# Input transposes of a and b side by side on two 64-row tiles of TensorE, 4 KB rows, and a part of the gate products on GpSimd: one change to a tuned scan and mixture-of-adapters kernel

## The chip, the cores and the metric

The kernel runs on one core of one Trainium2 chip. The metric is the device time of one execution in microseconds (us). One execution of each kernel was also taken with a profile; its "span" is the time from the first to the last instruction of the core, about 2 us less than the device time. In its lines PE is TensorE and PEld its weight load, DVE is VectorE, ACT ScalarE, POOL GpSimd and SP the engine that issues the transfers; a q marks the sequencer of an engine, which waits and issues. SBUF is the on-chip memory, whose tensors have up to 128 partitions in these kernels, and PSUM is the memory into which their matmuls write. The "granted clock" is the share of its full clock that the profile records for TensorE. Executions have a faster and a slower state, and only fast runs are compared here. A kernel that was run only once has the state "unknown"; it is used where the effect is many times the scatter of the runs, and marked where it is not.

## The reference

Two inputs `a` and `b` of 8 x 6400 x 128 float32 are scanned along the 6400 positions. The 51200 resulting rows `x` of 128 values then go through a mixture of eight rank-16 adapters, of which each row uses its two best.

```python
h = np.zeros((B, D))
for t in range(S):                 # scan: h = a*h + b, for 8 sequences
    h = a[:, t] * h + b[:, t]
    out[:, t] = h
x = out.reshape(B * S, D)          # 51200 x 128
logits = x @ w_gate                # 8 experts
topk = np.argpartition(-logits, 2, axis=1)[:, :2]
w = softmax of the two selected logits
delta[rows of e] += w * ((x @ A[e]) @ B[e])      # rank 16
return x + delta
```

## The kernel before

The rows are worked on in 100 units of 512 tokens. The scan is written with time along the free dimension and the 128 channels on the partitions, but the inputs lie in memory with a token's 128 channels together. So each unit goes through these steps; the letters are used throughout:

- A and B: TensorE transposes the unit's `a` and `b` (4 + 4 float32 matmuls against an identity, 128 x 128 each). ScalarE copies `a` from PSUM to SBUF.
- scan: VectorE runs the scan, which writes `xT` in float16.
- L: TensorE computes the logits (4 matmuls with 8 columns). GpSimd and VectorE compute the gates for a group of units.
- Z: TensorE computes x·A for all eight experts at once (4 matmuls). The product of Z with the gates runs on VectorE.
- T: TensorE transposes the product; R adds x into the output's PSUM tile and D adds the product times B. ScalarE copies the result, and a DMA stores it.

In L, Z and R the *stationary* operand, which TensorE loads as weights, is a block of `xT`. Partition p of a load holds four consecutive tokens, so a block consists of every fourth token, and its weight load reads `xT` with a step of 4 elements, which is 8 bytes.

All operations are listed with their dependences, and a small list scheduler inside the kernel puts them in order on each engine. The numbers in `KEY` are sort keys that were tuned for the kernel before.

```python
Q = 4; UT = 128 * Q; RING = 16            # 4 tokens a row, 512 tokens a unit
...
# load: one transfer over 128 partitions, two units, runs of 2 KB
ring[:, s0 : s0 + n, :],
rows[u0 * UT : (u0 + n) * UT, :].rearrange("(n p i) d -> p n (i d)", p=128, i=Q),
...
# A, B: four full transposes each
view = dst[:, :].rearrange("d (p i) -> d i p", i=Q)
for i in range(Q):
    last = h.transpose(view[:, i, :], ring[:, w % RING, i * 128 : (i + 1) * 128], ident_f[:, :])
...
def x_block(w, i):                        # weights of L, Z and R
    x0 = (w % XR) * UT
    return xT[:, x0 : x0 + UT].rearrange("d (p i) -> d i p", i=Q)[:, i, :]
...
for i in range(Q):                        # L; Z and R look alike
    last = h.matmul(pL[:, c : c + E], x_block(w, i), wg_h)
```

## Time and profile before

| | before |
|---|---|
| time, median of 3 runs | 211.31 us (211.17 to 211.38) |
| span of the profiled run | 209.4 us |
| busy: TensorE / VectorE / ScalarE / GpSimd | 97% / 92% / 81% / 42% |
| DMA rate from 60 to 180 us | 398 GB/s |
| TensorE time for a unit, 60 to 180 us | 1.91 us |

The TensorE time for a unit is, here and below, TensorE's busy time in the stretch, divided by the number of its matmuls there and multiplied by the matmuls of a unit (28 before, 36 after).

From the page of the kernel before come these lines: the busy times (PEld overlaps PE: 202.2 and 194.9 us in a span of 209.4), the moved GB/s in 40 equal slices of the span, the DMA queue of loads and stores (packets, MB, share of the 16 engines' time), and the chain of waits by engine.

```profile
PE 202.2 (97%) x2842; PEld 194.9 (93%) x2842; DVE 193.6 (92%) x279; ACT 170.2 (81%) x356; POOL 87.1 (42%) x190
...
GB/s 172 388 387 385 389 383 386 385 391 392 398 391 394 399 396 398 401 396 403 391 403 397 399 403 397 398 404 391 398 405 397 405 395 397 402 400 344 237 269 269
...
q1 hardware_dynamic: 40848, 78.65, 99.8%
...
PE 87%; DVE 6%; ACT 2%; issue 2%; POOL 0%; DVEq 0%; POOLq 0%
```

TensorE, VectorE and the DMA queue are all nearly full. The chain that ended last is TensorE for 87%. The DMA reaches its rate in the second slice and keeps it until nearly 190 us.

The next lines are groups of instructions of the kernel before: line, engine, operation, output and inputs, count | busy us, mean ns of one | idle time ahead and what ended it. The first is the transposes of `a`. The others are weight loads: those of R (L598), Z (L521) and L (L406) read `xT`, and that of D (L610) reads `zwT`.

```profile
L350 PE MATMUL pA<-ident_f,a_in 128*128 128x128 f32 x400 | 62.2, 279 | 0.8 <-ACT a_st L364 0.6
...
L598 PEld LDWEIGHTS pO<-ident_h,xT 128*128 128x128 f16 x400 | 30.1, 114 | 0.6 <-ACT outt L626 0.3
L610 PEld LDWEIGHTS pO<-cst_h,zwT 128*128 128x128 f16 x400 | 27.3, 98 | 2.3 <-PE pO L598 0.9
L521 PEld LDWEIGHTS pZ<-cst_h,xT 128*128 128x128 f16 x400 | 28.7, 114 | 0.2
...
L406 PEld LDWEIGHTS pTL<-cst_h,xT 128*128 128x128 f16 x400 | 20.5, 117 | 0.8 <-DVE xT L381 0.8
```

The DMA issues of the kernel before (KB each, median us from issue to landing):

```profile
a_in<-in_a_dram SPq DMA_DIRECT2D x49, 512.0 KB, 11.4
b_in<-in_b_dram SPq DMA_DIRECT2D x49, 512.0 KB, 11.4
```

### The profile page before, as it was taken

To read this page: it belongs to the slowest core of one execution; us is meant where nothing else is said; L and a number is where in the kernel's file an instruction comes from. 1 tells how busy PE (TensorE), PEld (TensorE's weight loads), DVE (VectorE), ACT (ScalarE), POOL (GpSimd) and SP (SyncE) were. 2 spreads that over 40 slices of the span, in tenths; PEclk is the share of its full clock that TensorE was granted. 3 is DMA by queue.
4 is the path that set the end of the run, shared out by engine and by line. 5 is a ranking of instruction groups with operands and counts; after the bars stand their busy time and mean duration, and the time that the engine had idled before them with its cause. 6 is when DMAs were issued, how large, how long until landed. Compare 5 with 4: busy or idle time off the path is not lost.

```text
span 209.4 us, 7147 instructions
## 1 busy us (share of the span) xinstructions
PE 202.2 (97%) x2842; PEld 194.9 (93%) x2842; DVE 193.6 (92%) x279; ACT 170.2 (81%) x356; POOL 87.1 (42%) x190
## 2 busy tenths in 40 slices
PE   6989999999999999999999999999999999999992
PEld 4779899999999999999999999999999999999991
DVE  1599999999999999999999999999999999999980
ACT  2437587779888889978979789988998899899993
POOL 1032715063335443563362545435453654354310
PEclk9999999999999999999999999999999999999999
DMA  7999999999999999999999999999999999999677
GB/s 172 388 387 385 389 383 386 385 391 392 398 391 394 399 396 398 401 396 403 391 403 397 399 403 397 398 404 391 398 405 397 405 395 397 402 400 344 237 269 269
DMA packets 42208, 79.23 MB, mean 378 GB/s; under 512 B 3648, under 2 KB 3776, under 8 KB 42176
## 3 DMA queue, kind: packets, MB, share of 16 engines
q1 hardware_dynamic: 40848, 78.65, 99.8%
q8 instruction: 22, 0.36, 0.7%
q10 hardware_dynamic: 1328, 0.14, 0.5%
q14 instruction: 10, 0.08, 0.1%
HBM read 52.56 MB, written 26.21 MB: 376 GB/s over the span
## 4 chain that ended last, share of the span: by engine, by line
PE 87%; DVE 6%; ACT 2%; issue 2%; POOL 0%; DVEq 0%; POOLq 0%
PE pA L350 20%; PE pB L350 19%; PE pO L610 11%; PE pZ L521 10%; PE pO L598 10%; PE pTL L571 10%; DVE xT L381 6%; PE pTL L406 5%; ACT a_st L364 1%; ACT outt L626 1%; PE pB L300 0%; PE pB L303 0%; ACT zwT L590 0%; PE pA L571 0%; PE pB L312 0%
## 5 line engine op out<-in xcount | busy, mean ns | idle before, releaser
L381 DVE TENSOR_TENSOR_SCAN xT<-a_st,xT,pB 128x512 f16<-128x512 f32 x96 | 120.2, 1252 | 2.7 <-PE pB L350 1.1
L364 ACT COPY a_st<-pA 128x512 f32<-128x512 f32 x100 | 59.7, 597 | 18.0 <-PE pA L350 10.7
L555 DVE TENSOR_TENSOR zw<-pZ,g 128x512 f16<-128x512 f32 x100 | 66.9, 674 | 0.8 <-ACT a_st L364 0.2
L626 ACT COPY outt<-pO 128x512 f32<-128x512 f32 x98 | 57.8, 594 | 10.5 <-PE pO L610 9.1
L350 PE MATMUL pA<-ident_f,a_in 128*128 128x128 f32 x400 | 62.2, 279 | 0.8 <-ACT a_st L364 0.6
L350 PE MATMUL pB<-ident_f,b_in 128*128 128x128 f32 x400 | 61.7, 277 | 0.2
L590 ACT COPY zwT<-pTL 128x512 f16<-128x512 f16 x95 | 56.5, 595 | 3.5 <-PE pTL L571 1.9
L350 PEld LDWEIGHTS pB<-ident_f,b_in 128*128 128x128 f32 x400 | 44.1, 142 | 1.8 <-issue 1.1
L350 PEld LDWEIGHTS pA<-ident_f,a_in 128*128 128x128 f32 x400 | 43.3, 143 | 1.8 <-issue 1.3
L610 PE MATMUL pO<-cst_h,zwT 128*128 128x128 f16 x400 | 38.8, 219 | 0.4
L598 PE MATMUL pO<-ident_h,xT 128*128 128x128 f16 x400 | 38.7, 219 | 0.1
L521 PE MATMUL pZ<-cst_h,xT 128*128 128x128 f16 x400 | 38.6, 219 | 0.0
L571 PE MATMUL pTL<-ident_h,zw 128*128 128x128 f16 x380 | 36.7, 219 | 0.0
L598 PEld LDWEIGHTS pO<-ident_h,xT 128*128 128x128 f16 x400 | 30.1, 114 | 0.6 <-ACT outt L626 0.3
L610 PEld LDWEIGHTS pO<-cst_h,zwT 128*128 128x128 f16 x400 | 27.3, 98 | 2.3 <-PE pO L598 0.9
L521 PEld LDWEIGHTS pZ<-cst_h,xT 128*128 128x128 f16 x400 | 28.7, 114 | 0.2
L571 PEld LDWEIGHTS pTL<-ident_h,zw 128*128 128x128 f16 x380 | 25.7, 98 | 0.3
L406 PE MATMUL pTL<-cst_h,xT 128*128 128x8 f16 x400 | 22.0, 174 | 0.3 <-DVE xT L381 0.3
L406 PEld LDWEIGHTS pTL<-cst_h,xT 128*128 128x128 f16 x400 | 20.5, 117 | 0.8 <-DVE xT L381 0.8
L449 POOL TENSOR_TENSOR d_1<-Lg,m_1 128x128 f32<-128x128 f32 (+2 forms) x13 | 5.1, 390 | 32.6 <-DVE m_1 L441 32.6
L449 POOL TENSOR_TENSOR d_0<-Lg,m_0 128x128 f32<-128x128 f32 (+1 forms) x12 | 4.8, 398 | 29.4 <-DVE m_0 L441 29.4
L381 DVE TENSOR_TENSOR_SCAN xT<-a_st,pB 128x512 f16<-128x512 f32 (+1 forms) x8 | 7.5, 942 | 5.7 <-PE pB L350 5.4
(58 smaller groups left out, 129.9 us busy)
## 6 DMA issues: line engine op xcount, KB each, us to landing
a_in<-in_a_dram SPq DMA_DIRECT2D x49, 512.0 KB, 11.4
b_in<-in_b_dram SPq DMA_DIRECT2D x49, 512.0 KB, 11.4
out_dram<-outt SPq DMA_DIRECT2D x49, 512.0 KB, 11.4
a_in<-in_a_dram SPq DMA_DIRECT2D x2, 256.0 KB, 3.6
b_in<-in_b_dram SPq DMA_DIRECT2D x2, 256.0 KB, 4.0
out_dram<-outt SPq DMA_DIRECT2D x2, 256.0 KB, 2.6
cst_f<-in_moe_A_dram ACTq DMA_DIRECT2D x1, 64.0 KB, 3.9
cst_f<-in_moe_B_dram ACTq DMA_DIRECT2D x1, 64.0 KB, 4.5
```

Source lines behind the costliest of these rows:

```text
L350: last = h.transpose(view[:, i, :], ring[:, w % RING, i * 128 : (i + 1) * 128], ident_f[:, :])
L364: lambda h: h.copy(a_st[w % 2][:, :], pA[:, :]),
L381: last = h.tensor_tensor_scan(out=xT[:, x0 + lo : x0 + hi], data0=a_st[w % 2][:, lo:hi], data1=pB[w % 2][:, lo:hi], initial=init, op0=ALU. ...
L406: last = h.matmul(pL[:, c : c + E], x_block(w, i), wg_h)
L449: lambda h: h.tensor_tensor(out=v(d1[s]), in0=v(Lg[s]), in1=bc(m1[s]), op=ALU.subtract),
L521: last = h.matmul(pZ[w % NZ][:, i * 128 : (i + 1) * 128], x_block(w, i), Acat_h)
L555: lambda h: h.tensor_tensor(out=oview, in0=zview, in1=gview, op=ALU.mult),
L571: last = h.transpose(t_dst(w)[:, i * 128 : (i + 1) * 128], zw[w % 2][:, i, :], ident_h[:, :])
L590: lambda h: h.copy(zwT[w % 2][:, :], t_dst(w)),
L598: last = h.matmul(pO[w % NO][:, i * 128 : (i + 1) * 128], x_block(w, i), ident_h[:, :], start=i == 0, stop=False, skip_group_check=True,)
L610: last = h.matmul(pO[w % NO][:, i * 128 : (i + 1) * 128], zwT[w % 2][:, i * 128 : (i + 1) * 128], Bcat_h, start=False, stop=True, skip_gro ...
L626: return copy(outt[:, w % NOUT, :], pO[w % NO][:, :])
```

## The change

The intent: a float32 transpose of 64 x 64 on one half of TensorE's rows runs beside another one on the other half. The warm-up of the kernel before shows it: at 2.72 us and at 2.73 us two of them start on the two halves, and the next two at 2.83 us. If unit w's `a` lies on one half of the partitions and its `b` on the other, `a` and `b` are transposed at the same time, in about half the time. For that a row holds 8 tokens (4 KB) instead of 4, a pair of units fills the 128 partitions, and `b` is loaded into the half opposite to `a`. VectorE, the next fullest engine (92%), hands 26 of the 100 gate products to GpSimd; GpSimd's product is written to read Z from SBUF, so ScalarE copies it there first. The sort keys were tuned anew. This is the core of the diff, with cuts marked:

```diff
-    Q = 4
-    UT = 128 * Q
-    RING = 16
+    Q = 8
+    HQ = Q // 2
+    UT = 64 * Q
+    RING = 8
...
+    ON_POOL = lambda v: 8 < v < NU - 12 and v % 3 == 1
...
+        def load(n):
+            s0 = n % RING
+            la = [(a_in[64 * h : 64 * h + 64, s0, :], a_rows[n, h, :, :]) for h in range(2)]
+            lb = [(b_in[64 - 64 * h : 128 - 64 * h, s0, :], b_rows[n, h, :, :]) for h in range(2)]
...
+            if n < 2:
+                for h in range(2):
+                    add_dma(f"ld{2 * n + h}", "sp", unit + h, [la[h], lb[h]], ("i", n, h), size, old)
+            else:
+                whole = (a_in[:, s0, :], a_rows[n].rearrange("h p f -> (h p) f"))
+                add_dma(f"lda{n}", "sp", unit, [whole], ("a", s0), size, old)
+                add_dma(f"ldb{n}", "sp", unit, lb, ("b", s0), size, old)
...
-                for i in range(Q):
-                    last = h.transpose(
-                        view[:, i, :], ring[:, w % RING, i * 128 : (i + 1) * 128], ident_f[:, :]
-                    )
+                for i in range(Q):
+                    c = slice(i * D, (i + 1) * D)
+                    for half, dst, ring in ((ha, da, a_in), (hb, db, b_in)):
+                        rows = slice(half, half + 64)
+                        last = h.transpose(dst[:, i, :], ring[rows, n, c], ident_f[rows, rows])
...
+        def x_block(v, q):
+            i = (v % 2) * HQ + q
+            return x_cols(v // 2).rearrange("d (p i) -> d i p", i=Q)[:, i, :]
+
+        def scanned(v):
+            return f"scan{v // 2 * 2 + 1}"
```

`lb` has two entries, so each `b` load is two transfers of 64 partitions, while `a` is one transfer of 128 (except for the first two pairs, which load both by halves). And `scanned` makes the output side of a unit wait for the scans of both units of its pair.

## The prediction

The 410 GB/s for rows of 4 KB, from which the 192 us of DMA time and with them the span of about 201 us come, was the author's estimate, and the kernel before had moved 398 GB/s. The sum for the main risk came to about 250 us. The 0.053 us of a pair is the 0.105 us of the warm-up scaled by full transposes, which in the trace of before start every 213 ns in the first 7.6 us and every 109 ns from 9 us on. A "change" (of mode) is one between 64-row transposes and matmuls on the whole array; the estimate of 0.1 us for it was from the 0.13 us of the warm-up.

> **What bounds the kernel now.** Three resources run nearly level. (1) DMA: the page's queue part gives 78.65 MB, busy 99.8%; the slices show 385 to 405 GB/s until about 185 us. In SP's timeline issues take 0.4 us at the start, 1.2 us later, and a transfer lands 11.4 us after issue: the queue is full. At 398 GB/s (stretch 60 to 140 us) one 512-token unit (0.786 MB) costs 1.97 us. (2) TensorE: the chain of waits is 87% PE; a unit costs 0.44 (A) + 0.44 (B) + 4 x 0.22 + 0.125 = 1.89 us. (3) VectorE: scan 1.19, product 0.60, reduces 0.13 = 1.93 us. ScalarE: 1.6 us per unit. After the last load (185 us) some 22 us of drain follow.
>
> **What the change does.**
> - TensorE: 16 half-height transposes in pairs replace 8 full ones. In the warm-up of before, a 64-row pair starts every 0.105 us[...], so 0.053 us warm: 8 pairs = 0.43 us instead of 0.88. [...]the warm-up shows about 0.13 us extra per change[...]. The order of instructions has 94 transpose groups, so 188 changes; at an estimated 0.1 us, 19 us. TensorE falls to about 1.65 us per unit.
> - VectorE loses 26 of 100 products (16 us): 1.77 us per unit. GpSimd gains 26, about 1.15 us each (estimate: 0.46 us for a quarter of the elements now), off the path. ScalarE gains 26 copies: 1.72 us.
> - DMA: same bytes, rows of 4 KB instead of 2 KB. A 2 KB packet takes 84 ns (packet records).[...]
>
> **On the critical path.** All engines drop below the DMA, so TensorE's gain of some 25 us is mostly hidden; DMA decides: 78.65 MB at 410 GB/s = 192 us, 2.5 us of start, and a drain that leaves about 7 us of DMA time unused (before: 12 us of the span in all). Span about 201 us, time about 203 us: 4% faster.
>
> **Main risk.** Each b load is two transfers of 64 partitions.[...] If both halves run at half rate throughout, [...]the kernel takes about 250 us[...]. I give a visible loss one chance in five.
>
> **What would show each step.** Right: transpose groups of about 0.45 us; PE's share of the chain well under 87%, with DMA waits in it; VectorE busy about 177 us, ScalarE 186, GpSimd 117; slices at 405 to 415 GB/s. Wrong: GB/s under 390 in the middle, b loads landing much later than a loads[...]; gaps over 0.15 us at mode changes (TensorE stays the limit); VectorE idle on GpSimd products; slices near 398 (packet size did not matter: about 207 us).
>
> **What would make it wrong.** [...]dearer mode changes, ScalarE becoming the limit, or a better drain (196).
>
> Time 203 us, range 196 to 218; faster 0.66, same 0.15, slower 0.19.

## The result, and the profile after

| | before | after |
|---|---|---|
| time, median | 211.27 us (4 runs beside it: 211.17 to 211.38) | 270.11 us (4 runs: 267.06 to 273.11) |
| fast runs of the changed kernel | | 267.06 and 268.13 us |
| ratio of fast runs, 95% interval | | 1.267 (1.262 to 1.271): slower |
| span of the profiled run | 209.4 us | 265.3 us |
| DMA rate from 60 to 180 us | 398 GB/s | 316 GB/s |

A ratio in this document is the mean time of one kernel's fast runs over that of the other's in the same rounds, so it is not quite the ratio of the quoted medians. Two of the four runs (273.11 and 272.08) fell in the slow state and are left out of it. The profiled run is the fastest one.

The same lines of the page, of the kernel after:

```profile
PE 217.3 (82%) x3605; PEld 196.2 (74%) x3605; DVE 185.0 (70%) x252; ACT 185.6 (70%) x380; POOL 111.4 (42%) x207
...
GB/s 136 217 258 273 263 245 246 232 261 284 305 250 311 335 326 300 349 339 322 351 314 300 312 361 324 308 300 324 325 350 351 332 329 349 369 387 330 214 250 233
...
q1 hardware_dynamic: 22576, 78.66, 97.6%
...
DMA 49%; PE 38%; SPq 7%; issue 3%; ACT 2%
```

The DMA queue is busy for 97.6% of a span that is 56 us longer, with the same 78.66 MB. So its engines are occupied all the time and move less: about 250 GB/s in the early slices, and only slowly more. TensorE fell from 97% to 82% busy, and the chain of waits is now half DMA.

The groups of the kernel after that answer to those shown of before, with one of the transposes and the new GpSimd product:

```profile
L362 PE MATMUL pA<-ident_f,a_in 64*128 64x64 f32 x800 | 78.7, 245 | 37.8 <-DMA a_in<-in_a_dram 27.9
...
L595 POOL TENSOR_TENSOR zw<-z_sb,g 128x512 f16<-128x512 f32 x26 | 27.6, 1061 | 45.9 <-PE pTL L611 16.7
...
L641 PEld LDWEIGHTS pO<-ident_h,xT 128*128 128x128 f16 x400 | 34.6, 152 | 2.4 <-ACT outt L673 0.2
L557 PEld LDWEIGHTS pZ<-cst_h,xT 128*128 128x128 f16 x400 | 34.4, 151 | 1.8 <-POOL d_0 L533 0.7
...
L443 PEld LDWEIGHTS pTL<-cst_h,xT 128*128 128x128 f16 x400 | 29.3, 162 | 0.7 <-DVE xT L407 0.2
L653 PEld LDWEIGHTS pO<-cst_h,zwT 128*128 128x128 f16 x400 | 27.6, 102 | 1.9 <-PE pO L641 0.6
```

TensorE waits 27.9 us for input loads ahead of its transposes of `a`; before, all its idle time there came to 0.8 us, and the wait named is for ScalarE. The weight loads from `xT` went from 114 to 117 ns up to 151 to 162 ns, while the contiguous one stayed near 100.

The DMA issues of the kernel after:

```profile
b_in<-in_b_dram SPq DMA_DIRECT2D x100, 256.0 KB, 17.5
out_dram<-outt SPq DMA_DIRECT2D x49, 512.0 KB, 18.7
a_in<-in_a_dram SPq DMA_DIRECT2D x48, 512.0 KB, 19.6
```

Everything lands late, the `a` loads a little later than the `b` loads. So the name in a wait ("DMA a_in") does not tell which transfer was the slow one: all of them are in one queue, q1.

The packet records give it a size. In the kernel before, a 2 KB packet takes 84 ns in the median (81 at the least) and 86.5 ns on average. In the kernel after, 4 KB packets take 156 ns at the least, 159 ns where nothing disturbs them (e2_b_whole below), but 213.7 ns on average, and a quarter take over 264 ns. The mean follows if the third of the packets that belongs to `b` takes double and the rest 159 ns: (159 + 159 + 318) / 3 = 212 ns. That is arithmetic on the sum; single packets were not told apart by their transfer.

Where the 55.9 us of span came from, by the starts of the transposes of unit 10 and of unit 99 in the traces:

| span, us | before | after | difference |
|---|---|---|---|
| up to unit 10 | 21.3 | 32.8 | +11.5 |
| unit 10 to unit 99 | 171.8 | 211.3 | +39.5 |
| unit 99 to the end | 16.3 | 21.1 | +4.8 |

### The profile page after: what moved, and what is told of

The parts are those of the page before. It is cut to its first block, busy times and chain, and to the rows that moved or that the text cites. A ratio compares the mean times of both kernels' runs of the same rounds, so it can differ in the third digit from the quotient of the medians.

```text
span 265.3 us, 8714 instructions
## 1 busy us (share of the span) xinstructions
PE 217.3 (82%) x3605; PEld 196.2 (74%) x3605; DVE 185.0 (70%) x252; ACT 185.6 (70%) x380; POOL 111.4 (42%) x207
## 3 DMA queue, kind: packets, MB, share of 16 engines
q1 hardware_dynamic: 22576, 78.66, 97.6%
## 4 chain that ended last, share of the span: by engine, by line
DMA 49%; PE 38%; SPq 7%; issue 3%; ACT 2%
DMA a_in<-in_a_dram 49%; PE pA L362 11%; SPq L267 7%; PE pO L641 6%; PE pZ L557 6%; PE pTL L611 5%; PE pO L653 5%; PE pTL L443 4%; PE pB L362 1%; ACT outt L673 1%; ACT zwT L633 1%; PE pA L611 0%; ACT Lg L476 0%; ACT g L550 0%
## 5 line engine op out<-in xcount | busy, mean ns | idle before, releaser
L362 PE MATMUL pA<-ident_f,a_in 64*128 64x64 f32 x800 | 78.7, 245 | 37.8 <-DMA a_in<-in_a_dram 27.9
L362 PEld LDWEIGHTS pA<-ident_f,a_in 64*128 64x128 f32 x800 | 63.9, 153 | 47.3 <-DMA a_in<-in_a_dram 32.4
L362 PE MATMUL pB<-ident_f,b_in 64*128 64x64 f32 x800 | 78.6, 245 | 0.1
L595 DVE TENSOR_TENSOR zw<-pZ,g 128x512 f16<-128x512 f32 x74 | 50.4, 682 | 26.1 <-PE pTL L611 23.3
L362 PEld LDWEIGHTS pB<-ident_f,b_in 64*128 64x128 f32 x800 | 63.9, 153 | 1.9 <-issue 1.9
L595 POOL TENSOR_TENSOR zw<-z_sb,g 128x512 f16<-128x512 f32 x26 | 27.6, 1061 | 45.9 <-PE pTL L611 16.7
L641 PE MATMUL pO<-ident_h,xT 128*128 128x128 f16 x400 | 45.1, 239 | 0.0
L611 PE MATMUL pTL<-ident_h,zw 128*128 128x128 f16 x380 | 39.5, 229 | 2.8 <-issue 2.1
L443 PE MATMUL pTL<-cst_h,xT 128*128 128x8 f16 x400 | 31.4, 200 | 0.7 <-issue 0.7
L443 PEld LDWEIGHTS pTL<-cst_h,xT 128*128 128x128 f16 x400 | 29.3, 162 | 0.7 <-DVE xT L407 0.2
L581 ACT COPY z_sb<-pZ 128x512 f32<-128x512 f32 x26 | 15.5, 594 | 0.4 <-PE pZ L557 0.4
## 6 DMA issues: line engine op xcount, KB each, us to landing
b_in<-in_b_dram SPq DMA_DIRECT2D x100, 256.0 KB, 17.5
a_in<-in_a_dram SPq DMA_DIRECT2D x48, 512.0 KB, 19.6
```

The lines of the kernel that those rows point to most:

```text
L362: last = h.transpose(dst[:, i, :], ring[rows, n, c], ident_f[rows, rows])
L443: last = h.matmul(pL[:, c : c + E], x_block(v, q), wg_h)
L595: lambda h: h.tensor_tensor(out=oview, in0=zview, in1=gview, op=ALU.mult),
L611: last = h.transpose(t_dst(v)[:, q * 128 : (q + 1) * 128], zw[v % 2][:, q, :], ident_h[:, :])
L641: last = h.matmul(pO[v % NO][:, q * 128 : (q + 1) * 128], x_block(v, q), ident_h[:, :], start=q == 0, stop=False, skip_group_check=True,)
```

## The experiments

The theory to begin with (theory P in the expectations): two transfers to opposite halves of the partitions are slow because of the partitions that each of them covers. Why these partitions should matter was the author's assumption; no trace shows it. The range 32 to 95, as large as a half but across both, is there to test the partition numbers alone. The rivals: the 4 KB rows or the memory's order of access; the larger number of transfers; TensorE's mode changes; GpSimd. Twelve kernels were run. All ratios are against the kernel before on the same chip, which took 210.9 to 211.7 us in all but one of its runs (213.6). Differences between two changed kernels go across chips in places, e6_blocks and e7_unpaired against e3_b_shift above all; the kernel before took the same time on these chips to 0.3 us in the median. Several of the expectations missed: e2_b_whole and e4_b_mid lay between the two ranges given for them, e3_b_shift and e11_order_a above both; e1_before_b_halves and e14_two_switches came out 2 to 3 us over theirs, and e6_blocks 0.2 us under.

### e2_b_whole: b as one transfer over 128 partitions

This kernel is wrong on purpose: the halves of `b` arrive swapped. Its instructions on the compute engines have the same order as those of the kernel after.

```diff
-                add_dma(f"ldb{n}", "sp", unit, lb, ("b", s0), size, old)
+                whole_b = (b_in[:, s0, :], b_rows[n].rearrange("h p f -> (h p) f"))
+                add_dma(f"ldb{n}", "sp", unit, [whole_b], ("b", s0), size, old)
```

> The changed kernel with each b load of a pair of units as ONE transfer of 128 partitions instead of two of 64. The order of instructions on PE, DVE, ACT and POOL is the same; the halves of b land swapped, so the result is wrong on purpose. Theory P ([...]the 4 KB packets double from 159 ns towards 318 ns): about 200 to 208 us, mean 4 KB packet 159 to 165 ns, 405 to 415 GB/s in the middle. Rival H (rows of 4 KB, or the HBM addresses they touch, are slow): stays at 260 to 270 us. Rival E (mode changes of TensorE, the products on GpSimd, or the ring of 8 pairs hold the pipeline): stays at 260 to 270 us, for those are untouched.

Measured: 228.0 us, 39 us less than the fastest run of the kernel after. The slices of its page:

```profile
GB/s 123 221 325 405 414 403 411 409 398 409 415 411 412 413 414 413 414 411 412 413 412 416 411 411 416 412 399 382 408 414 412 411 256 169 66 175 126 221 281 188
```

The rate in the middle is 411 GB/s, above the 398 of before, and 4 KB packets take 166.9 ns on average. So 4 KB rows are not the cause; they are even a little better. But 228 us is still 17 us more than before: a second loss lies beneath the first.

### e4_b_mid and e5_b_apart: the same two transfers, on the middle partitions or on the two halves

Both are wrong on purpose: `b` is loaded into two buffers, and the transposes read `a` in place of `b`. They differ in two lines and have the same order of instructions on every engine, the same number of transfers and the same bytes. e5_b_apart is the control.

```diff
 # e4_b_mid                                  # e5_b_apart
-(b_in[32:96, s0, :], b_rows[n, 0, :, :]),
-(b_lo[32:96, s0, :], b_rows[n, 1, :, :]),
+(b_in[64:128, s0, :], b_rows[n, 0, :, :]),
+(b_lo[0:64, s0, :], b_rows[n, 1, :, :]),
```

> The changed kernel with the two 64-partition b loads of each pair kept in number, size and HBM rows, but both put on partitions 32 to 95 (in two buffers)[...]. The transposes read a's buffer in place of b's (wrong result on purpose; b is loaded and waited for, and not read). Theory P: about 200 to 210 us, packets near 159 ns. Rival N (a transfer of 64 partitions or 256 KB, or twice as many transfers, is slow[...]): 260 to 270 us.

> Control of the run on partitions 32 to 95: the same kernel, order and buffers, but the two b transfers on partitions 64 to 127 and 0 to 63 as in the changed kernel. Theory P: 260 to 275 us, mean 4 KB packet over 200 ns. If it is as fast as its sibling, the edit (reading a's buffer, the extra buffer) removed the loss[...].

Measured: 232.65 us on partitions 32 to 95, and 273.57 us on 64 to 127 and 0 to 63. The slices of e4_b_mid and then of e5_b_apart:

```profile
GB/s 119 221 325 409 410 406 410 410 410 407 413 413 413 403 414 397 398 373 392 412 408 419 397 408 409 408 390 380 378 412 383 415 209 168 91 183 119 163 273 186
```

```profile
GB/s 137 218 250 270 259 252 238 223 274 259 298 241 300 333 311 335 341 318 315 314 314 330 326 345 344 323 289 323 333 322 320 297 283 308 343 386 333 206 204 262
```

The number of transfers, the size of each, the rows and the work of all engines are the same; only the partition numbers differ, and 41 us go with them. The mean 4 KB packet is 168.6 against 219 ns. From 60 to 180 us e4_b_mid moved 401 GB/s, against 411 in e2_b_whole. This settles the main cause: it is the partitions that one transfer covers, not that there are two transfers. Why such a pair on the two halves is slow was not shown.

### e1_before_b_halves: the cause alone, in the kernel before

Only the `b` loads of the kernel before are cut into two transfers of 64 partitions. The result is correct.

```diff
+                for lo in ((0, 128),) if t == "a" else ((64, 128), (0, 64)):
+                    p = slice(*lo)
...
-                            rows[...].rearrange("(n p i) d -> p n (i d)", p=128, i=Q),
+                            rows[...].rearrange("(n p i) d -> p n (i d)", p=128, i=Q)[p],
```

> The kernel before, whole, except that each b load is cut into two transfers, partitions 64 to 127 and then 0 to 63 (2 KB rows, same bytes, right result). Nothing else of the change is in it. Theory P[...]: clearly slower, 240 to 275 us, many 2 KB packets near 168 ns instead of 84. If the loss needs the 4 KB rows or another part of the change: 211 to 216 us.

Measured: 277.18 us, 66 us more than before. Its slices and its chain of waits:

```profile
GB/s 182 264 269 237 251 246 225 225 279 212 254 252 250 276 293 282 335 355 322 311 303 299 305 303 308 324 302 288 298 289 338 331 301 345 299 363 391 318 260 233
...
DMA 67%; PE 23%; SPq 4%; issue 2%; ACT 2%; DVE 0%; ACTq 0%
```

The slices have the shape of those of the kernel after: near 250 GB/s at first, then slowly more. The mean 2 KB packet is 115.3 ns; with the third of the packets at double time it would be (84 + 84 + 168) / 3 = 112. One part of the change, alone, costs at least as much as the whole change did (this is a single run of unknown state, so the 10 us more are not read). No mode change outside the warm-up, no GpSimd product and no 4 KB row is in this kernel.

### e3_b_shift: a correct kernel with whole `b` loads

If `b` is shifted by one unit, its first half-tile holds unit 0 alone, and from then on units 2m-1 and 2m lie together, on the halves where they are wanted. One transfer over 128 partitions then loads both.

```diff
-                add_dma(f"ldb{n}", "sp", unit, lb, ("b", s0), size, old)
+                load_b(n)
+        def load_b(m):
...
+                rows = b_units[2 * m - 1 : 2 * m + 1].rearrange("u p f -> (u p) f")
+                src, size = (b_in[:, m % RING, :], rows), 2 * UT * D * 4
```

> A correct repair: b's tiles are shifted by half a tile (512 tokens), so that one transfer of 128 partitions brings unit 2m-1 to partitions 0 to 63 and unit 2m to 64 to 127; a and b of a unit still lie in opposite halves. All of the change's other parts stay. Theory P: 198 to 206 us, faster than before by 3 to 6%, DMA at 405 to 415 GB/s and still the limit. If TensorE's mode changes or ScalarE limit the rest: 207 to 215 us with DMA slices under 400 GB/s.

Measured: 224.39 us (222.85 to 225.28), ratio 1.061 (1.056 to 1.067), correct. The stretch from 60 to 180 us of the kernels before, after and e3_b_shift, in this order (busy us and number of instructions of PE, PEld, DVE, ACT, POOL, then granted clock, DMA share, GB/s):

```profile
60.00:180.00 120.00, 120.00 (x1760) 118.77 (x1758) 118.03 (x164) 105.62 (x223) 57.31 (x116) 1.00 1.05 398
```

```profile
60.00:180.00 120.00, 102.14 (x1794) 93.44 (x1793) 88.25 (x112) 93.47 (x192) 62.90 (x110) 0.97 1.04 316
```

```profile
60.00:180.00 120.00, 119.96 (x2207) 111.72 (x2206) 106.66 (x134) 113.02 (x236) 73.93 (x128) 1.00 1.03 413
```

With the half transfers gone from this stretch, TensorE is full again, for 120 of 120 us, and the DMA moves 413 GB/s. A unit costs TensorE 1.96 us, against 1.91 before. So the side-by-side transposes did not make TensorE faster over a whole unit, and the chain that ended last is TensorE again:

```profile
PE 84%; DVE 6%; DMA 4%; SPq 2%; ACT 2%; issue 1%; DVEq 0%
```

By the starts of its instructions in this stretch, a unit consists of 8 pairs at 62 ns (0.50), of which the second starts 50 ns later than that (0.05), the two gaps at mode changes (0.19), R and Z with 8 matmuls at 62 to 63 ns (0.50), T and D with 8 at 56 ns (0.45) and L with 4 at 60 ns (0.24): 1.93 us, and the rest is waits and R and Z steps above their median. Before, the sum was 8 transposes at 109 ns (0.87), 16 matmuls at 56 ns (0.90) and L with 4 at 33 ns (0.13): 1.90 us. A gain of 0.37 us on the transposes is used up by 0.24 us of mode changes (the 0.19 and the 0.05 us at the second pair), 0.05 us or more on R and Z, and 0.11 us on L.

The timeline of TensorE in one unit of before and of e3_b_shift (start us, us, engine, line and operation, count) shows the steps:

```profile
100.93 0.39 PE L598 MATMUL pO<-ident_h,xT 128*128 128x128 f16 x4
101.16 0.27 PE L406 MATMUL pTL<-cst_h,xT 128*128 128x8 f16 x4
101.29 0.39 PE L521 MATMUL pZ<-cst_h,xT 128*128 128x128 f16 x4
```

```profile
100.46 0.22 PE L378 MATMUL pA<-ident_f,a_in 64*128 64x64 f32 x1
100.52 0.22 PE L378 MATMUL pB<-ident_f,b_in 64*128 64x64 f32 x1
100.52 0.22 PE L378 MATMUL pA<-ident_f,a_in 64*128 64x64 f32 x1
100.68 0.40 PE L627 MATMUL pTL<-ident_h,zw 128*128 128x128 f16 x4
...
101.14 0.36 PE L459 MATMUL pTL<-cst_h,xT 128*128 128x8 f16 x4
101.36 0.43 PE L657 MATMUL pO<-ident_h,xT 128*128 128x128 f16 x4
...
101.85 0.43 PE L573 MATMUL pZ<-cst_h,xT 128*128 128x128 f16 x4
102.21 0.27 PE L378 MATMUL pA<-ident_f,a_in 64*128 64x64 f32 x1
...
102.32 0.22 PE L378 MATMUL pA<-ident_f,a_in 64*128 64x64 f32 x1
...
102.39 0.22 PE L378 MATMUL pA<-ident_f,a_in 64*128 64x64 f32 x1
```

From one start to the next: the four L matmuls take 0.13 us before and 0.22 in e3_b_shift. A pair follows the last one after 0.06 us, but the first full-array matmul follows the last transpose only after 0.16 us. In the stretch the medians are 155 ns from a transpose to a full matmul (59 inside the transposes) and 156 ns from Z to a transpose (62 inside Z): each mode change costs about 95 ns in its gap, which is what the prediction had taken. One step later stands another 50 ns: the second pair of a group starts 112 ns after the first, every later one 62 ns after the last (102.21, 102.32 and 102.39 us above). So a unit pays 0.24 us for its two changes, which makes some 23 us for 94 groups of transposes. The warm-up of the kernel before shows it too, with 0.16 us to the second pair and 0.105 us from then on. (The busy times of a matmul, 0.2 to 0.4 us here, overlap and are not its cost.)

### e6_blocks: weights without a step

This kernel is e3_b_shift with contiguous weight blocks in L, Z and R. It is wrong on purpose: the blocks hold the wrong tokens. The order of instructions is the same on every engine.

```diff
-            return x_cols(v // 2).rearrange("d (p i) -> d i p", i=Q)[:, i, :]
+            return x_cols(v // 2)[:, i * 128 : (i + 1) * 128]
```

> The shifted-b repair (224.4 us), but each 128-column block of xT that TensorE loads as weights is contiguous instead of taken every 8th element (16 bytes); wrong result on purpose (rows permuted), same order of instructions on every engine. Theory S (8 tokens per partition row made the weight loads of L, Z and R slower: a logits matmul starts every 60 ns instead of 33, R and Z every 63 to 71 instead of 56): L back to 33 to 40 ns, R and Z to 56, about 0.2 us less TensorE time per unit, then the DMA at 413 GB/s limits at 1.90 us per unit: 214 to 220 us. Rival (the slower L, Z, R are an effect of mode changes or waits nearby): cadences stay and so does the time, 222 to 226 us.

Measured: 213.84 us, 10.5 us less than e3_b_shift. The weight loads from `xT` in e3_b_shift, and then in e6_blocks:

```profile
L573 PEld LDWEIGHTS pZ<-cst_h,xT 128*128 128x128 f16 x400 | 33.9, 150 | 1.0 <-DVE zw L611 0.2
...
L459 PEld LDWEIGHTS pTL<-cst_h,xT 128*128 128x128 f16 x400 | 29.1, 163 | 0.7 <-DVE xT L423 0.2
```

```profile
L573 PEld LDWEIGHTS pZ<-cst_h,xT 128*128 128x128 f16 x400 | 25.8, 99 | 3.6 <-issue 1.5
...
L657 PEld LDWEIGHTS pO<-ident_h,xT 128*128 128x128 f16 x400 | 24.6, 98 | 4.3 <-issue 1.3
```

They take 97 to 99 ns now, as every contiguous one. L matmuls start every 25 ns, R and Z every 56, and a unit costs TensorE 1.78 us. So the step of the weights is the second loss. The three steps side by side: contiguous 97 to 99 ns (e6_blocks), 8 bytes 114 to 117 ns (before), 16 bytes 150 to 163 ns (e3_b_shift). The L matmuls, of only 8 columns, started every 25, 33 and 60 ns there.

### e7_unpaired: is the pairing worth anything?

This kernel is e3_b_shift with the eight transposes of `a` first and then the eight of `b`, so that neighbours use the same half.

```diff
-                for i in range(Q):
-                    c = slice(i * D, (i + 1) * D)
-                    for half, dst, ring, slot in ((ha, da, a_in, n), (hb, db, b_in, m)):
+                for half, dst, ring, slot in ((ha, da, a_in, n), (hb, db, b_in, m)):
+                    for i in range(Q):
+                        c = slice(i * D, (i + 1) * D)
```

> The shifted-b repair with the 16 half-height transposes of a unit issued as 8 of a and then 8 of b, so that neighbours use the same 64-row tile[...]. Theory T (the pairing itself works, 62 ns per pair, and its gain is eaten by mode changes and strided weights): the 16 take 0.9 to 1.8 us instead of 0.55, TensorE is the limit at 2.3 us or more per unit: 250 us or more. If pairing brought nothing: 222 to 228 us.

Measured: 260.5 us, 36 us more than e3_b_shift. TensorE needs 2.27 us for a unit, since neighbouring transposes on one half start 62 to 63 ns apart, one at a time, where e3_b_shift starts a pair every 62 ns. The pairing of the change works as intended.

### e10_units_start: small steps, whole loads at the start

This kernel is e3_b_shift with three edits: the first loads also cover 128 partitions, the output side goes by units of 512 tokens (so it waits for one scan, not two), and a weight block takes every fourth token again (8 bytes), for which stores use 2 KB rows.

```diff
-            i = (v % 2) * HQ + q
-            return x_cols(v // 2).rearrange("d (p i) -> d i p", i=Q)[:, i, :]
+            x0 = v % (2 * XR) * UT
+            return xT[:, x0 : x0 + UT].rearrange("d (p i) -> d i p", i=HQ)[:, q, :]
...
-            return f"scan{v // 2 * 2 + 1}"
+            return f"scan{v}"
```

> A version meant to beat both: b shifted; loads in 4 KB rows and whole 128-partition transfers from the first pair on (only the first 512 tokens of b are a half); everything after the scan by units of 512 tokens with 4 tokens per output row as before (weights every 8 bytes, stores in 2 KB rows). Right result. Theory ([...]strided weights + slow start are what the repair still lost): start of the 11th unit's transposes near 21 us instead of 30, L at 33 ns, PE about 1.8 us per unit, DMA about 1.93 us per unit: 203 to 210 us. If TensorE's mode changes or the schedule still hold it: 211 to 220 us.

Measured: 215.28 us (213.73 to 216.58), ratio 1.015 (1.007 to 1.022), unclear by the 2% rule, correct. A unit costs TensorE 1.82 us; L starts every 33 ns and R and Z every 56, as before. With 89 units from unit 10 to unit 99 this takes 165.5 us instead of 171.8, so in the middle this kernel is 6.3 us faster than before. But unit 10 starts 5.6 us later (26.9 against 21.3), and the end comes 22.4 us after the start of unit 99 instead of 16.3. The gain in the middle is given back at the two ends.

### e11_order_a and e12_order_b: other orders

Both have the edits of e10_units_start, and other sort keys, group sizes and cost estimates in the scheduler, and 20 of the products on GpSimd (the expectation says 22), from a search with the kernel's own list scheduler.

```diff
-        "AB": -40.4, "aev": -12.4, "scan": 1.4, "L": -4.4, "lev": -7.7, "gate": -0.8, "sig": -36.0, "Z": 10.2,
+    KEY = {'AB': 7.7, 'aev': 39.5, 'scan': 28.7, 'L': -99.0, ...}           # e11_order_a
+    KEY = {'AB': -174.9, 'aev': -154.6, 'scan': 21.5, 'L': -45.3, ...}      # e12_order_b
+    ON_POOL = lambda v: 8 < v < NU - 14 and v % 4 == 1
```

> The version of shifted b, whole first loads and unit-wise output (215.3 us) with another order of instructions (new sort keys, 22 instead of 26 products on GpSimd, other tail groups); right result. That version ran 1.86 us per unit in the middle, against 1.93 before, but lost 5.6 us at the start and 6 us after the last transposes. If the order is what costs there: 204 to 210 us, faster than before by 1 to 3%. If start and tail are set by the longer chain from load to store: 211 to 216 us.

> A second order of instructions for the same version, more transposes first. Same expectation: 204 to 210 us if the order costs, 211 to 216 us if not.

Measured: e11_order_a 223.62 us, ratio 1.059 (1.056 to 1.063); e12_order_b 212.82 us (211.14 to 212.84), ratio 1.004 (1.000 to 1.009). The order and the group sizes alone are worth 11 us here. e12_order_b is the best version found and equals the kernel before by the 2% rule; no version beat it. In e12_order_b the middle is 9.0 us faster than before (162.8 against 171.8), the start 6.0 us slower and the tail 4.6 us slower.

### e13_no_pool: all products on VectorE

This kernel is e10_units_start with no product on GpSimd.

```diff
-    ON_POOL = lambda v: 8 < v < NU - 12 and v % 3 == 1
+    ON_POOL = lambda v: False
```

> The same version (215.3 us) with all gate products on VectorE. VectorE then has 1.93 us of work per unit against 1.77. Theory (the GpSimd part of the change works and is needed once DMA and TensorE are below 1.9 us): 218 to 224 us, VectorE busy over 195 us and nearly without idle time. If it brings nothing: 213 to 217 us.

Measured: 221.11 us in a single run, about 6 us more than the 215.28 of e10_units_start, whose four runs reach to 216.58. VectorE is busy 195.9 us instead of 184.5. So the hand-over to GpSimd probably helps once the other limits are gone. This is not more than probable: the 6 us are only twice the scatter of e10_units_start, and the order was not tuned anew for this kernel, where an order alone was worth 11 us above. That the hand-over did not cause the loss is shown elsewhere: e2_b_whole and e4_b_mid keep it and take 39 and 34 us less than the kernel after, and e1_before_b_halves has none of it and shows the loss.

### e14_two_switches: two more mode changes for each unit

This kernel is e3_b_shift with one full-array matmul of 8 columns in the middle of each unit's transposes. What it writes is overwritten by the next transposes, so the result stays correct.

```diff
                 for i in range(Q):
+                    if i == HQ:
+                        h.matmul(da[:, Q - 1, 0:8], warm_t[:, 0:128], warm_t[:, 0:8])
                     c = slice(i * D, (i + 1) * D)
```

> The shifted-b repair (224.4 us, TensorE the limit at 1.97 us per unit) with one matmul of 8 columns on the whole array put into the middle of each unit's transposes, so that each unit has two more changes of tiling mode; its 8 columns are overwritten by the transposes that follow, so the result is right. Theory M (a change of mode costs about 95 ns of TensorE time, and TensorE is the limit there): 0.19 to 0.25 us more per unit, 243 to 250 us. If changes of mode are hidden or TensorE is not the limit: 224 to 230 us.

Measured: 253.29 us, 28.9 us more than e3_b_shift, and 3 us over the top of what was expected. Its timeline around the extra matmul:

```profile
101.96 0.22 PE L380 MATMUL pB<-ident_f,b_in 64*128 64x64 f32 x1
102.11 0.18 PE L376 MATMUL pA<-warm_t 128*128 128x8 f16 x1
102.23 0.27 PE L380 MATMUL pA<-ident_f,a_in 64*128 64x64 f32 x1
...
102.34 0.22 PE L380 MATMUL pA<-ident_f,a_in 64*128 64x64 f32 x1
...
102.40 0.22 PE L380 MATMUL pA<-ident_f,a_in 64*128 64x64 f32 x1
```

From the last transpose to the matmul the median is 156 ns and from there to the next transpose 114 ns, where 59 ns stood: 211 ns for a unit, or 21 us for 100 units. The pair after that is 50 ns late as well (102.23, 102.34 and 102.40 us above), which makes 0.26 us for a unit or 26 us, and TensorE's time for a unit is indeed 2.22 us instead of 1.96. So mode changes do cost TensorE's time in full, here 0.13 us each with the extra matmul itself. Some 3 us of this run stay open.

## Why the prediction was wrong, point by point

**The step that failed: "I give a visible loss one chance in five."** The prediction named the cause, and even its size: about 250 us in case that the halves run at half rate. It then gave that case one chance in five, in the hope that the halves would overlap and cost little. What failed is that hope: the cost did not hide behind the rest of the queue. The whole queue moved 316 GB/s from 60 to 180 us where the prediction counted on 410. e4_b_mid against e5_b_apart shows that the cost is there, 41 us, and that it hangs on the partition numbers alone. e1_before_b_halves shows that this one cause suffices for the whole loss. Removing it from the changed kernel in a correct way (e3_b_shift) brings the time from 267 to 224 us. The runs show that such a pair is slow (273.57 us against 232.65); how far its two transfers overlap was not measured. The hope had nothing measured behind it, since no load or store of the kernel before covered a half.

There may be a grain of truth in the hope: the rate of the kernel after rises from about 250 GB/s in the early slices to over 330, so the loss does shrink. The traces also show the first and the last of the 16 landings of one `a` transfer moving apart, from under 4 us in the first 50 us to 5 to 7 us from 94 to 151 us and 8 to 12 us after that. But they move apart in the kernel before as well, from 0.4 to 5.6 us. That this is what raises the rate was not tested. Up to 225 us no slice passed 361 GB/s.

**The sign named for it was half wrong.** "GB/s under 390 in the middle" was seen (316). "b loads landing much later than a loads" was not: `a` landed after 19.6 us and `b` after 17.5. The transfers are in one queue, and in e1_before_b_halves, where only the `b` loads are cut, the weight loads of the transposes of `a` wait 20.3 us for loads of `a` as well, where before they waited for none.

**"TensorE falls to about 1.65 us per unit" was wrong** by 0.3 us. e3_b_shift needs 1.96, and takes 172.4 us from unit 10 to unit 99 where the kernel before takes 171.8: the whole gain expected in the middle is gone, even without the half transfers. Its terms: the pairs cost 0.50 us instead of 0.43; the mode changes 0.24 us instead of 0.19, since the late second pair was not counted; and the term that was left out, the weights' step of 16 bytes instead of 8, adds at least 0.16 us (L 0.11, R and Z 0.05 or more). (The 0.43 was scaled from the start of the trace of before: full transposes start every 213 ns there and every 109 ns later. The granted clock reads 1.00 at both times.) e6_blocks shows that the step is worth 10.5 us of the time. The kernel before's own profile had shown 114 to 117 ns against 98. Of its reason nothing is shown but the trend with the step: 97 to 99 ns contiguous, 114 to 117 with 8 bytes, 150 to 163 with 16.

**"All engines drop below the DMA ... DMA decides" was wrong** for the same reason. With the half transfers gone, TensorE and not the DMA was full for 120 of 120 us (e3_b_shift), and the time was again that of TensorE.

**The ends were mis-sized.** The prediction allowed 2.5 us of start and a drain with about 7 us of unused DMA time. e3_b_shift starts unit 10 8.5 us later than before and ends 4.1 us later after unit 99. Some of the start is again half transfers (its first four units come about 2.5 us apart, and 0.524 MB in 2.5 us is 210 GB/s); the contiguous weights of e6_blocks alone took back 2.2 us of it, and e10_units_start with whole loads, units and small steps 2.9. So e3_b_shift, at 224.39 us, owes its 6% over the kernel before almost wholly to the two ends. Which of the remaining differences, a single buffer for transposed `a`, the wait for both `a` and `b`, or the order, makes the rest of it was not separated.

**Right were:** the DMA rate with rows of 4 KB, 410 GB/s estimated against 411 to 413 with whole loads, where packets of 4 KB take 159 ns and those of 2 KB 84 before; about 0.1 us for the gap of a mode change; ScalarE at 186 us busy against 185.6; GpSimd at 117 against 111, with a product at 1.06 us instead of 1.15; and that the hand-over to GpSimd lies off the critical path (the chain of waits of the kernel after shows none of it). VectorE was predicted at 177 us and measured at 185. The lower granted clock of the kernel after (0.97 in the stretch) cannot explain its loss, since TensorE is idle for 18 of those 120 us; why it fell was not tried.

**Where the expected gain went.** Side-by-side transposes save 0.37 us of TensorE per unit. Without the half transfers, 0.24 us of that goes into mode changes and 0.16 us or more into the strided weights, which is all of it and a little more. With the small steps restored (e10_units_start, e12_order_b) TensorE's part of the middle does get faster than before, by 6 to 9 us over 89 units, and the start and the tail, 10 to 12 us longer, give it back.

## What to carry to other kernels

Count a load that is split over two halves of the partitions as two slow loads, unless a run shows otherwise (here 273.57 us against 232.65 with the same two transfers on partitions 32 to 95); a shift of the data by half a tile can turn them back into full-width ones (e3_b_shift, 267 to 224 us). When a layout grows the run length in memory, follow the new step to every reader, above all to the weight loads of many small matmuls, and look up in the profile what a step costs there already (here 114 to 117 ns against 98). And when a risk is named and sized, weigh it by what has been measured against it, which here was nothing.
